# Weight conversion in the mixed steps: words combined ahead of the queries, next mask last, cast behind the numerators

## The chip, the cores and the metric

The kernel runs on one core of a Trainium2 chip. A core has TensorE (matrix products, into PSUM), VectorE, ScalarE and GpSimd (element-wise work), each with an instruction queue of its own that is worked off in order, and SyncE, whose queue issues most DMAs. An instruction waits on semaphores until what it needs is done and what it overwrites has been read; everything behind it on its engine waits as well. The metric is device time in microseconds. TensorE's clock was granted in full (2.4 GHz) through the stretch that the change touches.

## The reference

Three parts follow each other. First, attention with a feature map, for 4 batches, 8 heads, 576 tokens and head size 64:

```python
def phi(x):
    proj = x @ w_phi                       # 64 -> 128
    proj = proj - max(abs(proj))
    return concat(exp(proj), exp(-proj))   # 256 features
kv  = sum over tokens of phi(k) * v;   z = sum over tokens of phi(k)
out = (phi(q) @ kv) / (phi(q) @ z + 1e-6)
```

Its 2304 x 512 output goes to a mixture of 8 experts with one expert per token (argmax of `x @ w_gate`, a capacity per expert, two layers with relu, 1024 wide, gate weight on the result). Then comes a dense layer, `h = x @ w_in` (2048 wide), `g = h - tanh(h)`, `g @ w_out`. The dense layer's weights are handed over as 64-bit floats.

## The kernel before

**Steps.** The attention part works on 18 chunks of 128 tokens. `attention()` has a loop over steps `s`. Step `s` takes chunk `i = s` through the key side, chunk `j = s - 5` through the query projection (LAG is 5) and chunk `jt = s - 6` through transposition, exponentials and numerators. So keys and queries mix from step 5 to step 17. One key chunk passes through:

- `proj("k", i)`: 16 small products into a PSUM pair (`xb`, in early odd steps `yb`), L306;
- `sub("k", i)`, VectorE: the largest magnitude of each head (reduce, L314), then the subtract (L317);
- `kexp(i)`, ScalarE: the two exponentials, L328 and L329;
- `vgate(i)`, 16 products, and `vcopy`, ScalarE: value columns for the gate;
- `kv_step(i)` in the next step: 64 products (L358) that add to the key-value sums. At the end of a batch of 576 tokens `kv_evac` copies the sums to SBUF (ScalarE, L368).

A query chunk passes through `proj("q", j)` into `xb`, `sub("q", j)`, `trans` into `yb`, `qexp` (ScalarE, L396), `num` (64 products, L457, into `yb`) and the copies of denominators and numerators to SBUF (ScalarE, L474 and L475); `xstore` sends the numerators to DRAM. In steps 9 to 17 VectorE also runs pieces of the routing (`route1`, small operations) for the nine early chunks. In steps 10, 13 and 16 ScalarE's exponential of the routing (L510) stands ahead of the numerators' copy.

**Weight conversion.** Beside this, the steps convert the dense layer's weights, 13 pieces of 128 x 1024 numbers (`pieces`; `CV` maps step 4 to piece 0, step 16 to piece 12). A 64-bit number comes as two 32-bit words, and a piece passes through:

- `cv_load`: four DMAs of 256 KB into `raw` (two buffers), L119;
- scaling, `cv_mag`, ScalarE: exponent and top bits of the high word as a 32-bit float, into `a` (two buffers), L93;
- mask, VectorE: the sign bit of the high word, into `m` (one buffer), L98;
- shift, VectorE: `a` moved left by 3 bits, L100;
- combine, VectorE: the low word's top bits joined to it, L102;
- add, GpSimd: the sign joined to it, L106;
- `cv_hi`, the cast, ScalarE: the rounded high part of the weight, L277;
- `cv_lo`, GpSimd: the low part, `a` minus the high part, L280.

**What sets the order.** The program is in a manual schedule: each engine's queue holds its instructions in the order in which the loop writes them. Before the change, a step's mask and shift stand behind the key subtract, the combine behind the routing at the end, the cast and `cv_lo` of a piece one step later, and the scaling of the next piece at the very end of the step.

## Time and profile before

| | us |
|---|---|
| median of 3 runs (lowest, highest) | 668.98 (668.04, 670.8) |
| profiled execution | 670.01 |
| its span | 668.3 |
| busy: TensorE, VectorE, ScalarE, GpSimd | 637.6, 524.1, 411.4, 240.5 |

The span is the time from the first to the last instruction, about 1.7 us less than the device time. The mixed steps lie between 24 and 141 us, with the weight conversion from 23 to 140; the rest is the late query steps, the experts and the dense layer. An instruction's length in the trace runs from its start on the engine to its end; a wait for a semaphore stands before the start, as idle time. Successive VectorE instructions overlap by about 0.1 us.

### The profile page before, as it was taken

The numbers are of one execution on the slowest core, as the hardware profiler recorded it, in microseconds if no ns is written. First come the engines' busy times: TensorE is split into PE (matmuls) and PEld (weight loads), VectorE is DVE, ScalarE is ACT, GpSimd is POOL, SyncE is SP. The second block draws the span as 40 slices with busy tenths as digits, with TensorE's granted clock in tenths as the row PEclk, the third lists the DMA queues.
The fourth block names the chain that finished last, engine by engine and source line by source line (L and its number), as shares of the span: only waits on it lengthen the run. The fifth ranks groups of instructions, "written<-read, shape, count | busy, mean of one in ns | idle before, by whom it ended". The sixth has DMA issues, their size and how long they took to land. (4 is left out here: it accounts for less than half of the span.)

```text
span 668.3 us, 17411 instructions
## 1 busy us (share of the span) xinstructions
PE 637.6 (95%) x7107; PEld 620.9 (93%) x7107; DVE 524.1 (78%) x772; ACT 411.4 (62%) x720; POOL 240.5 (36%) x182
## 2 busy tenths in 40 slices
PE   7999899998998999999999999999999999999993
PEld 6889888888988999999999999999999999999992
DVE  4799999997867888989865548889975637888982
ACT  3688868786635576576644446567745526657661
POOL 1255564546000326433720113633460102543361
PEclk9999999999999999999999999999999999999998
DMA  8988886726446424402235501001315530100221
GB/s 284 298 282 296 258 275 209 226 74 218 143 145 199 158 95 167 136 4 87 68 97 166 161 6 44 26 1 44 97 28 159 165 108 1 41 13 1 88 70 40
DMA packets 44922, 83.14 MB, mean 124 GB/s; under 512 B 7281, under 2 KB 7921, under 8 KB 44833
## 3 DMA queue, kind: packets, MB, share of 16 engines
q1 hardware_dynamic: 39664, 68.99, 32.8%
q0 software_dynamic: 2624, 8.13, 4.2%
q10 hardware_dynamic: 2544, 4.82, 2.0%
q8 instruction: 58, 0.95, 0.6%
q14 instruction: 32, 0.25, 0.1%
HBM read 73.32 MB, written 13.31 MB: 130 GB/s over the span
## 5 line engine op out<-in xcount | busy, mean ns | idle before, releaser
L1030 POOL TENSOR_SCALAR al<-ut 128x576 fp32r<-128x576 f32 (+1 forms) x51 | 84.1, 1650 | 151.8 <-ACT ut L1026 83.0
L925 DVE TENSOR_TENSOR w<-raw,w 128x512 fp32r<-128x512 f32 x102 | 71.7, 719 | 45.8 <-ACT w L920 43.7
L920 ACT CAST w<-raw 128x512 fp32r<-128x512 f32 x102 | 61.6, 619 | 62.3 <-DMA raw<-w 30.4
L938 PE MATMUL xb<-xh,w_in_h 128*128 128x288 f32 x264 | 79.5, 301 | 1.3 <-ACT ut L1026 1.3
L940 PE MATMUL xb<-xh,w_in_l 128*128 128x288 f32 x264 | 78.3, 297 | 0.0
L939 PE MATMUL xb<-xl,w_in_h 128*128 128x288 f32 x264 | 78.2, 296 | 0.0
L1077 POOL DMA_INDIRECT out<-row,ids x18 | 20.6, 1146 | 115.7 <-DVE row L1075 77.6
L1017 DVE TENSOR_TENSOR al<-y,ah 128x576 fp32r<-128x576 f32 (+1 forms) x51 | 40.5, 795 | 24.8 <-ACT ah L1016 24.7
L1025 ACT COPY hs<-xb 128x576 f32<-128x576 f32 (+1 forms) x36 | 21.6, 600 | 58.7 <-DVE th L1048 28.6
L939 PE MATMUL kvb<-al,w_oa_h 128*128 128x288 f32 x180 | 53.5, 297 | 0.0
L940 PE MATMUL kvb<-ah,w_oa_l 128*128 128x288 f32 x180 | 53.2, 296 | 0.0
L938 PE MATMUL kvb<-ah,w_oa_h 128*128 128x288 f32 x180 | 53.2, 296 | 0.0
L1041 DVE SCALAR_TENSOR_TENSOR y<-y,ut 128x576 f32<-128x576 f32 (+1 forms) x51 | 41.3, 811 | 13.4 <-ACT y L1029 13.4
L938 PEld LDWEIGHTS xb<-xh,w_in_h 128*128 128x128 f32 x264 | 49.8, 189 | 1.4 <-ACT ut L1026 1.4
L1044 DVE SCALAR_TENSOR_TENSOR y<-y,y 128x576 f32<-128x576 f32 (+1 forms) x51 | 44.2, 867 | 7.3 <-ACT y L1031 5.9
L939 PEld LDWEIGHTS xb<-xl,w_in_h 128*128 128x128 f32 x264 | 49.7, 188 | 0.0
L940 PEld LDWEIGHTS xb<-xh,w_in_l 128*128 128x128 f32 x264 | 49.6, 188 | 0.0
L314 DVE TENSOR_REDUCE m<-xb 128x8 f32<-128x1024 f32 x33 | 40.3, 1221 | 11.2 <-PE xb L306 10.7
L1049 DVE COPY_PREDICATED y<-al,th 128x576 f32<-128x576 int32 (+1 forms) x51 | 42.8, 840 | 5.6 <-DVE th L1048 0.5
L1031 ACT ACTIVATE y<-ut,sq_b 128x576 f32<-128x576 f32 (+1 forms) x51 | 38.1, 748 | 13.5 <-DVE al L1017 11.7
L938 PE MATMUL yb<-xh,w 128*128 128x288 f32 x144 | 43.8, 304 | 0.7 <-DVE al L985 0.7
L938 PE MATMUL kvb<-ah,w 128*128 128x288 f32 x144 | 42.6, 296 | 1.8 <-ACT ah L984 1.0
(291 smaller groups left out, 2136.5 us busy)
## 6 DMA issues: line engine op xcount, KB each, us to landing
raw<-w SPq DMA_DIRECT2D x105, 256.0 KB, 3.1
raw<-win SPq DMA_DIRECT2D x32, 256.0 KB, 4.5
raw<-wout SPq DMA_DIRECT2D x20, 256.0 KB, 4.6
v<-v SPq DMA_DIRECT2D x16, 296.0 KB, 4.0
k<-kT SPq DMA_DIRECT2D x18, 256.0 KB, 4.6
vt<-vT SPq DMA_DIRECT2D x18, 256.0 KB, 3.7
q<-qT SPq DMA_DIRECT2D x18, 256.0 KB, 4.2
xs<-x SPq DMA_DIRECT2D x18, 256.0 KB, 3.9
```

Of the source, the lines that this page charges most:

```text
L314: nc.vector.tensor_reduce(out=m, in_=ps, axis=AX.X, op=ALU.max, apply_absolute_value=True)
L920: nc.scalar.copy(d[:, 0], t)
L925: eng.tensor_tensor(out=d[:, 1], in0=t, in1=d[:, 0].bitcast(F32), op=ALU.subtract)
L938: nc.tensor.matmul(o, ah, bh, start=first, stop=False, skip_group_check=True)
L939: nc.tensor.matmul(o, ah, bl, start=False, stop=False, skip_group_check=True)
L940: nc.tensor.matmul(o, al, bh, start=False, stop=last, skip_group_check=True)
L1017: nc.vector.tensor_tensor(out=AL[a][:, i], in0=y2[:, i], in1=AH[a][:, i].bitcast(F32), op=ALU.subtract)
L1030: nc.gpsimd.tensor_scalar(out=AL[a][:, i], in0=ut[:, i], scalar1=C2, scalar2=None, op0=ALU.is_gt)
L1031: nc.scalar.activation(out=y2[:, i], in_=ut[:, i], func=AF.Square, bias=sq_b[:, 1:2])
L1041: nc.vector.scalar_tensor_tensor(out=y1[:, i], in0=y1[:, i], scalar=T1, in1=ut[:, i], op0=ALU.add, op1=ALU.mult)
L1044: nc.vector.scalar_tensor_tensor(out=y2[:, i], in0=y2[:, i], scalar=T2, in1=y1[:, i], op0=ALU.add, op1=ALU.mult)
L1049: nc.vector.copy_predicated(y2[:, i], AL[a][:, i].bitcast(I32), th[:, i])
```

## The change

The mask leaves `cv_bits` and becomes `cv_mask`. In step `s`, shift, combine and GpSimd's add of the step's own piece stand together behind the key subtract, ahead of the queries. The scaling of the next piece stands behind the key exponentials, the mask of the next piece behind the routing as the step's last VectorE instruction, and the cast and `cv_lo` of the step's own piece behind the numerators, ahead of `vgate` and `vcopy`. The loads move too: a piece's first two DMAs are issued in the middle of a step (from step 4 on), the other two at the top of the next one.

```diff
--- before.py
+++ after.py
@@ -94,9 +94,6 @@
 
     def cv_bits(t, a, m=None):
 
-        if m is not None:
-            nc.vector.tensor_scalar(out=m, in0=t[:, :, 1], scalar1=SIGN, scalar2=None, op0=ALU.bitwise_and)
-            yield
         nc.vector.tensor_scalar(out=a, in0=a, scalar1=3, scalar2=None, op0=ALU.logical_shift_left)
         yield
         nc.vector.scalar_tensor_tensor(out=a, in0=t[:, :, 0], scalar=29, in1=a,
@@ -266,9 +263,13 @@
         def cv_mag(i):
             if i in raw:
                 a = cva[i] = cv.tile([P, NPC], I32, tag="a", name="a")
-                m = cvm[i] = cv.tile([P, NPC], I32, tag="m", name="m", bufs=1)
                 cvw[i] = a.bitcast(F32)
                 cv_size(raw[i], a)
+
+        def cv_mask(i):
+            if i in raw:
+                m = cvm[i] = cv.tile([P, NPC], I32, tag="m", name="m", bufs=1)
+                nc.vector.tensor_scalar(out=m, in0=raw[i][:, :, 1], scalar1=SIGN, scalar2=None, op0=ALU.bitwise_and)
 
         def cv_main(i):
             yield from cv_bits(raw.pop(i), cva.pop(i), cvm.pop(i))
@@ -761,7 +762,7 @@
             i, j, jt = s, s - LAG, s - LAG - 1
             jn = jt if s < SD else jt - 1 if s > SD else -1
             kk, qq, tt = i < NCH, 0 <= j < NCH, 0 <= jt < NCH
-            pc, pd = CV.get(s), CV.get(s - 1)
+            pc, pn = CV.get(s), CV.get(s + 1)
             since = {cs: s - (cs[-1] + LAG + 1) for cs in subs}
             if s == SK:
                 stk.close()
@@ -772,11 +773,9 @@
             if kk:
                 proj("k", i, xb if i > LAG or i % 2 == 0 else yb)
             if s >= LAG:
-                cv_load(s + 2 - LAG, 0, 1)
+                cv_load(s + 2 - LAG, 2, 3)
             if s + 2 < NCH:
                 ldk(s + 2)
-            if s >= LAG:
-                cv_load(s + 2 - LAG, 2)
             if kk:
                 if i < LAG:
                     vgate(i)
@@ -791,29 +790,28 @@
             if kk:
                 for _ in sub("k", i):
                     pass
-            bits = iter(()) if pc is None else cv_main(pc)
-            run(itertools.islice(bits, 2))
+            if pc is not None:
+                run(cv_main(pc))
             if qq:
                 proj("q", j, xb)
             if 0 <= j + 2 < NCH:
                 ldq(j + 2)
-            if s >= LAG:
-                cv_load(s + 2 - LAG, 3)
-            else:
+            if s < LAG:
                 for k in ((0, 1), (2, 3), (4, 5), (6,), (7,))[s]:
                     cv_load(k // 4, k % 4)
+            if s >= LAG - 1:
+                cv_load(s + 3 - LAG, 0, 1)
             if i - 1 in strad:
                 kv_second(i - 1)
             if i == NCH:
                 kv_step(i - 1)
                 first_ids()
-            if pd is not None:
-                cv_hi(pd)
-                cv_lo(pd)
             if kk:
                 kexp(i)
                 if i < LAG and i in strad:
                     vcopy(i, 1)
+            if pn is not None:
+                cv_mag(pn)
             wgen = iter(())
             if since[subs[-1]] == 3:
                 wgen = itertools.chain(route2(early), table(early))
@@ -836,14 +834,15 @@
                 smalls.append(fgen["u"])
             weave([], smalls)
             flush()
-            for _ in bits:
-                pass
+            if pn is not None:
+                cv_mask(pn)
             if 0 <= jn < NCH:
                 num(jn)
+            if pc is not None:
+                cv_hi(pc)
+                cv_lo(pc)
             if LAG <= i < NCH:
                 vgate(i)
-            if CV.get(s + 1) is not None:
-                cv_mag(CV[s + 1])
             if s == SK:
                 mo["first"]()
             if s + 2 < NCH:
```

The lines of the changed kernel are numbered a little differently: mask L272, shift L97, combine L99, reduce L315, subtract L318.

On VectorE, around steps 4 to 6, the queue before stood as follows; `raw_209` and `a_410` belong to piece 0, `raw_338` and `a_485` to piece 1, `yb` with L314 and L317 is the key chunk of step 5, and the first `xb` here is the first query chunk.

```order
L98 TENSOR_SCALAR m_411<-raw_209 128x1024
L100 TENSOR_SCALAR a_410<-a_410 128x1024
L102 SCALAR_TENSOR_TENSOR a_410<-raw_209,a_410 128x1024
L314 TENSOR_REDUCE m_540<-yb_85 128x8
L317 TENSOR_TENSOR d_542<-yb_85,m_540 128x1024
L98 TENSOR_SCALAR m_486<-raw_338 128x1024
L100 TENSOR_SCALAR a_485<-a_485 128x1024
L314 TENSOR_REDUCE m_594<-xb_84 128x8
L317 TENSOR_TENSOR d_596<-xb_84,m_594 128x1024
L102 SCALAR_TENSOR_TENSOR a_485<-raw_338,a_485 128x1024
```

The same stretch of VectorE's queue in the changed kernel, where `a_488` is piece 1's and `raw_480` piece 2's:

```order
L97 TENSOR_SCALAR a_410<-a_410 128x1024
L99 SCALAR_TENSOR_TENSOR a_410<-raw_209,a_410 128x1024
L272 TENSOR_SCALAR m_490<-raw_338 128x1024
L315 TENSOR_REDUCE m_544<-yb_85 128x8
L318 TENSOR_TENSOR d_546<-yb_85,m_544 128x1024
L97 TENSOR_SCALAR a_488<-a_488 128x1024
L99 SCALAR_TENSOR_TENSOR a_488<-raw_338,a_488 128x1024
L315 TENSOR_REDUCE m_601<-xb_84 128x8
L318 TENSOR_TENSOR d_603<-xb_84,m_601 128x1024
L272 TENSOR_SCALAR m_605<-raw_480 128x1024
```

The mask of piece 1 moved ahead of step 5's key reduce, and the combine of piece 1 from behind the first queries to ahead of them.

On ScalarE, step 6 before, from the query exponentials; `w_in_h` is the cast, `x` the numerators, `a_748` the scaling of the next piece.

```order
L396 ACTIVATE qp_639<-yb_85 128x1024 x2
L277 CAST w_in_h_65<-a_485 128x1024
L328 ACTIVATE kp_693<-d_676 128x8x128
L329 ACTIVATE kp_693<-d_676 128x8x128
L474 COPY dl_734<-yb_85 128x72
L475 COPY x_735<-yb_85 128x2x4x64
L337 CAST v1_152<-ones_123 128x8
L338 COPY v1_152<-sb_80 128x8x8
L93 ACTIVATE a_748<-raw_625 128x1024
```

The same step on ScalarE in the changed kernel (`a_701` is the next piece's scaling):

```order
L397 ACTIVATE qp_643<-yb_85 128x1024 x2
L329 ACTIVATE kp_698<-d_680 128x8x128
L330 ACTIVATE kp_698<-d_680 128x8x128
L93 ACTIVATE a_701<-raw_561 128x1024
L475 COPY dl_741<-yb_85 128x72
L476 COPY x_742<-yb_85 128x2x4x64
L278 CAST w_in_h_65<-a_599 128x1024
L338 CAST v1_152<-ones_123 128x8
L339 COPY v1_152<-sb_80 128x8x8
```

The scaling moved from behind `vcopy` to ahead of the numerators' copy, and the cast from ahead of the key exponentials to between that copy and `vcopy`.

## Rows read from the trace of the kernel before

In the first group the columns are: stretch, its length, then busy us and instructions (x) of TensorE's products, its weight loads, VectorE, ScalarE and GpSimd, the granted clock, the busy share of the DMA engines and GB/s. In the groups in order of time they are: start and length in us, engine (DVE is VectorE, ACT ScalarE, POOL GpSimd, PE TensorE), line, operation, output and inputs, shapes and types, count, and in brackets the idle time just before with what ended it.

**Rows 1.** Busy times of the mixed steps, by engine (columns above).

```profile
24.00:135.00 111.00, 103.61 (x2366) 96.22 (x2362) 105.81 (x132) 86.86 (x138) 59.01 (x27) 1.00 0.81 260
```

**Rows 2.** VectorE in order of time: start, length, engine, line, operation.

```profile
26.22 1.23 DVE L102 SCALAR_TENSOR_TENSOR a<-raw,a 128x1024 int32<-128x1024 int32 x1
27.36 1.22 DVE L314 TENSOR_REDUCE m<-yb 128x8 f32<-128x1024 f32 x1
...
30.00 0.69 DVE L98 TENSOR_SCALAR m<-raw 128x1024 int32<-128x1024 int32 x1
...
31.21 1.22 DVE L314 TENSOR_REDUCE m<-xb 128x8 f32<-128x1024 f32 x1
32.46 1.23 DVE L317 TENSOR_TENSOR d<-xb,m 128x1024 f32<-128x1024 f32 x1
33.61 2.23 DVE L102 SCALAR_TENSOR_TENSOR a<-raw,a 128x1024 int32<-128x1024 int32 x1
35.76 1.21 DVE L314 TENSOR_REDUCE m<-xb 128x8 f32<-128x1024 f32 x1
...
59.80 1.22 DVE L314 TENSOR_REDUCE m<-xb 128x8 f32<-128x1024 f32 x1
...
64.12 1.23 DVE L314 TENSOR_REDUCE m<-xb 128x8 f32<-128x1024 f32 x1 [0.56 <-PE xb L306]
...
67.06 2.14 DVE L501 TENSOR_TENSOR lgx<-dl,r 128x192 f32<-128x192 f32 x1
...
77.20 0.18 DVE L508 TENSOR_TENSOR ls<-lg,mx 128x24 f32<-128x24 f32 x1
...
89.96 1.15 DVE L98 TENSOR_SCALAR m<-raw 128x1024 int32<-128x1024 int32 x1
...
94.56 0.36 DVE L501 TENSOR_TENSOR lgx<-dl,r 128x192 f32<-128x192 f32 x1
...
103.24 1.45 DVE L508 TENSOR_TENSOR ls<-lg,mx 128x24 f32<-128x24 f32 x1
...
134.49 1.21 DVE L314 TENSOR_REDUCE m<-xb 128x8 f32<-128x1024 f32 x1
```

**Rows 3.** GpSimd in order of time, the same columns.

```profile
27.60 2.37 POOL L106 TENSOR_TENSOR a<-a,m 128x1024 int32<-128x1024 int32 x1 [5.70 <-DVE a L102]
32.38 2.37 POOL L280 TENSOR_TENSOR w_in_l<-a,w_in_h 128x1024 fp32r<-128x1024 f32 x1 [2.41 <-ACT w_in_h L277]
...
89.99 0.58 POOL L240 MEMSET v<- 64x584 f32 x1
```

**Rows 4.** ScalarE in order of time, the same columns.

```profile
28.91 1.17 ACT L93 ACTIVATE a<-raw 128x1024 f32<-128x1024 f32 x1 [1.43 <-DMA raw<-win]
...
31.23 1.07 ACT L277 CAST w_in_h<-a 128x1024 fp32r<-128x1024 f32 x1
...
64.36 1.25 ACT L368 COPY kvs<-kvb 128x438 f32<-128x438 f32 x3
...
77.42 0.22 ACT L510 ACTIVATE ls<-ls 128x24 f32<-128x24 f32 x1 [1.64 <-DVE ls L508]
...
77.65 0.59 ACT L475 COPY x<-yb 128x512 f32<-128x512 f32 x1
```

**Rows 5.** TensorE in order of time: three key projections (steps 6, 8 and 9).

```profile
33.74 1.16 PE L306 MATMUL xb<-small,k 64*128 64x128 f32 x16 [0.32 <-DVE d L317]
...
50.51 1.16 PE L306 MATMUL xb<-small,k 64*128 64x128 f32 x16
...
58.59 1.16 PE L306 MATMUL xb<-small,k 64*128 64x128 f32 x16
```

**Rows 6.** Tile view of the weight words: time from issue to landing.

```profile
DMA to landing us min/median/max: 2.9/4.5/6.6
```

**Rows 7.** ScalarE's waits, 24 to 125 us: total, times, longest.

```profile
ACT a L93 <- DMA raw<-win: 6.4, 4, 2.2
ACT a L93 <- DMA raw<-wout: 3.9, 1, 3.9
```

## The prediction

> **What bounds the kernel now.** I read first the busy times of the stretch that the change touches, the mixed steps from 24 to 135 us [rows 1]. VectorE is busy 105.8 of its 111.0 us and TensorE 103.6, while ScalarE has 24 us of room and GpSimd 52. The reader should see two engines near their limit at once, and 533 us of the span behind it that the change leaves alone. Then I read VectorE's instructions in order of time [rows 2], which show the order of the work in a step and where one instruction takes longer than its like; then what ran on GpSimd and ScalarE at those moments [rows 3, 4]; then TensorE's step starts [rows 5]; last, the landing of the weight loads and who waits for them [rows 6, 7].
>
> Three things stand in them. A plain step takes TensorE 8.08 us from one key projection to the next (50.51 to 58.59) [rows 5]. VectorE and TensorE pass one PSUM pair (xb) to and fro: the next key projection starts when the query subtract ends (32.46 + 1.23 = 33.69, projection 33.74) [rows 2, 5]. And VectorE instructions that read SBUF wait for GpSimd: the word combine at 33.61 takes 2.23 us instead of the 1.23 at 26.22, and it ends 1.09 us after GpSimd's subtract, which runs from 32.38 for 2.37 us [rows 2, 3]. The reduce at 27.36, which reads PSUM, keeps its 1.22 us beside GpSimd's add that starts at 27.60.
>
> **The change part by part, in the profiled execution's own time.** Its device time is 670.01 us, its span 668.3; the median of the three runs is 668.98. I add a difference to both.
>
> *The lead-in, steps 4 to 6.* The mask of piece 0 moves into step 3, where VectorE has idle time, so combine 0 starts a mask's 0.60 earlier, at 25.62, and GpSimd's add, 1.38 behind it as before, runs 27.0 to 29.4 [rows 2, 3]. Now the mask of piece 1 stands behind combine 0 and ahead of step 5's key reduce. There is one mask buffer, which that add reads, and step 4 has no queries whose reduce and subtract (1.25 + 1.23) could cover the add. The mask therefore starts at 29.4, and the load of piece 1 lets it go no earlier than 28.9 either (ScalarE's scaling of the same words started at 28.91, after waiting for a DMA) [rows 4]. Behind it are queued the key reduce, now at 30.05 instead of 27.36, and the whole of step 5. The shift is due 2.64 later (27.36 to 30.00), at 32.7. But the cast of piece 0 now stands in step 4 behind that scaling (28.91 + 1.17, then 1.07), so GpSimd's subtract of piece 0 runs about 31.25 to 33.6, and the shift, an SBUF instruction, waits for it: 0.9. Then 0.60 shift (half of 30.00 to 31.21), 1.14 combine (26.22 to 27.36), 1.25 reduce and 1.23 subtract of the queries: the key projection of step 6 starts at 37.9 instead of 33.74. The key reduce comes 1.21 behind it (58.59 to 59.80), at 39.1 instead of 35.76. Sum: **+3.35 us**. The second half of the lead-in's loss is that the combine, which before ran beside the key projection, now stands ahead of it.
>
> *Steps 6 to 8, no routing.* The round over xb is 1.21 (projection to reduce) + 2.6 (to the shift) + 0.60 + 1.14 + 1.25 + 1.28 (subtract to projection) = 8.08, as long as TensorE's own 8.08. The mask (0.6) lies beside the key projection. Three such steps are 24.3 with the small gaps; before, 35.76 to 59.80 is 24.04 [rows 2]. Sum: **+0.3**.
>
> *Steps 9 to 16.* The add now runs beside the query reduce and subtract, which read PSUM, so the late instructions of this stretch lose their extra: 67.06 (2.14; its like at 94.56 takes 0.36: 1.78), 89.96 (1.15 for 0.69: 0.46), 103.24 (1.45, its like at 77.20 takes 0.18: 1.27), and one like that at 112.63 (1.15) [rows 2]. That is -4.7. Twice a query reduce waited 0.56 for TensorE (64.12 and one like it); the combine now fills that: -1.1. The last mixed step has no mask: -0.6. What is late next is the shift. The cast stands behind the numerators' copy, and that stands behind the routing exponential or the copy of the key-value sums. In a step with that exponential it is 0.82 from the exponential to the end of the numerators' copy (77.42 to 78.24), then the cast's 1.07, so GpSimd's subtract starts 2.0 after the exponential and ends 4.35 after it [rows 4]. VectorE needs 0.3 to finish routing, 0.6 for the mask, 1.3 and 1.2 for the next key reduce and subtract, so its shift is due at 3.4: it waits 0.9. The copy of the sums (1.25 at 64.36) puts the cast as far back. Two steps of each kind: +3.6, and +0.6 for small overlaps elsewhere. Sum: **-2.2**.
>
> *The loads.* Each piece's four DMAs move half a step forward on SyncE. The first two still wait for the combine and now stand behind the query load and ahead of the vt load; the last two no longer wait for VectorE. The scaling moves forward by about as much, so I cost this at 0; what it can cost is the slower rival, what it can gain the faster one. *After the mixed steps*, step 17 has no cast and subtract any more, and its exponentials start without a waiting cast ahead of them: **-0.2**.
>
> In all +3.35 + 0.3 - 2.2 - 0.2 = **+1.2 us**: 671.2 against the profiled execution, 670.2 against the median.
>
> The one term without a row of its own is the shift's wait. The rows show a two-input combine wait for GpSimd's subtract, and a one-input mask, the shift's like, wait for a GpSimd memset: the mask at 89.96 ends 0.54 after the memset (89.99 + 0.58) [rows 2, 3]. Bounds: nothing, or a whole subtract (2.37) each time. I take the overlap that the order leaves, 0.9, by the mask's row, the nearest. Without any wait, the five shifts would come 4.5 us earlier on VectorE; but TensorE's 8.08 and the xb round let only half of that through, about 2.3 us, and the sum would be -1.1. With a whole subtract each it would be some +4.
>
> The Trainium skill, SBUF — State Buffer, "Who interferes with whom", says that a tensor_scalar between SBUF operands can enter a two-port mode and then contends with GpSimd, whose instruction holds the shared pair to its end. The trace agrees on the mask (1.15 us); no row here shows the shift beside a GpSimd subtract. By that rule the shift waits and the sum is +1.2; by the memset's row read narrowly, where only a memset would hold it, -1.1.
>
> **The rivals.**
> 1. *The start is cheaper and the waits go.* The shifts do not wait, and words half a step earlier free the exponentials. For it: ScalarE waited 6.4 + 3.9 us for weight words [rows 7], ahead of query exponentials. Against it: VectorE is back to back from 26.22 to 35.76 [rows 2], so there is nowhere to catch up the mask's wait. Price: lead-in without the shift's wait +2.45, +0.3, and -6.4 in steps 9 to 16: -3.6, so 665.4.
> 2. *A new round through the loads makes it slower.* The scaling now stands ahead of the numerators' copy on ScalarE, and it needs words that SyncE issues behind the store of the previous copy. The round is two issues (0.9), the landing, the scaling (1.17), the copy (0.8) and the handing over (0.1): 3.0 us plus the landing. It decides from a landing of 5.1 us in a plain step (8.1), 5.7 in one with routing (8.7). For it: landings reach 6.6, and one scaling waited 3.9 [rows 6, 7]. Against it: the median is 4.5, and these two loads now stand where the first two stood. At 6.0 us the round is 9.0: three plain steps lose 0.9 each and some others 0.3, +3.3, so 673.5; at 6.6 it is 9.6, three lose 1.5 and seven 0.9, +10.8: 681.
> 3. *It comes out even.* Steps 9 to 16 pay back the lead-in because the casts hold the shifts half as long: +1.8 instead of +3.6, so 668.4.
>
> **How the numbers follow.** My forecast, +1.2 with a range of its own of -0.5 to +3, has 0.45; rival 1 has 0.15, rival 2 0.2, rival 3 0.2. The predicted time is 670.2 us. The range that should hold it 8 times in 10 stops a little short of rival 1's 665.4 and takes in the mild form of rival 2: 666.0 to 674.0. A measurement of this kernel tells about 0.5% (3.3 us) from no change: under 665.6 or over 672.3. Faster is rival 1 and little else: 0.14. Slower is rival 2 and the upper edge of the forecast: 0.24. The rest, 0.62, is the same.
>
> **What would show it.** In the changed profile the mask of piece 1 on VectorE starts near 29.4, with the key reduce of step 5 at about 30; if that stands near 27.4, the lead-in was wrong. The key projection of step 6 starts near 37.9. No combine takes over 1.3 us, while shifts of 1.3 to 1.9 us (mask and shift had 0.69 before) stand in the steps after an exponential or a copy of the sums; if they stay at 0.69, the +4.2 in steps 9 to 16 was wrong. Scaling that waits for a DMA in most steps, with the numerators' copy late behind it, would be rival 2. The key reduce of step 17 stands near 135.9 (134.49 before). The forecast is wrong as a whole if that instant moves by more than 3.3 us, or if the time from there to the end, 533.8 us before, changes by more than 1.

## The result and the profile after

The changed kernel takes **675.45 us** (median of 5 runs, 674.11 to 676.15); the kernel before, beside it, 668.21 (668.04 to 670.8). The ratio is 1.010, with a 95% interval of 1.008 to 1.012: slower by 7 us, outside the predicted range. The profiled execution took 674.11 us, its span is 672.4.

To see where the time went I cut the mixed steps at TensorE's key projections, which every kernel here has. All numbers are us from one start to the next, each from one profiled execution:

| kernel | steps 4-5 | 6-8 | 9-13 | 14-16 | sum |
|---|---|---|---|---|---|
| before | 12.61 | 24.85 | 45.39 | 27.86 | 110.71 |
| changed | 16.33 | 27.10 | 43.68 | 28.99 | 116.10 |
| difference | +3.72 | +2.25 | -1.71 | +1.13 | +5.39 |

The spans of these two executions differ by 4.1 us only, where the medians differ by 7.2: the profiled execution before is 1.8 above its median, the one after 1.3 below. Their 4.1 are 0.56 ahead of the table's first start, the table's 5.39, and -1.9 behind its last. Neither the first nor the last of these is read here as the work of the change. The first 20 us hold the same work in both kernels, and they differ between executions: step 4's projection starts at 21.13 before, at 21.69 here and at 23.61 in the repeat below, with a granted clock of 1.00, 0.70 and 0.50 from 12 to 16 us. So stretches are compared in what follows, and instants on the clock of the span only with that in mind.

First VectorE in the lead-in, in order of time; the rows that answer to it are [rows 2]. The columns of all rows in order of time are those of the rows before.

```profile
26.09 1.23 DVE L99 SCALAR_TENSOR_TENSOR a<-raw,a 128x1024 int32<-128x1024 int32 x1
29.88 0.69 DVE L272 TENSOR_SCALAR m<-raw 128x1024 int32<-128x1024 int32 x1 [2.56 <-POOL a L103]
30.49 1.22 DVE L315 TENSOR_REDUCE m<-yb 128x8 f32<-128x1024 f32 x1
...
32.95 1.36 DVE L97 TENSOR_SCALAR a<-a 128x1024 int32<-128x1024 int32 x1
34.35 1.22 DVE L99 SCALAR_TENSOR_TENSOR a<-raw,a 128x1024 int32<-128x1024 int32 x1
35.49 1.22 DVE L315 TENSOR_REDUCE m<-xb 128x8 f32<-128x1024 f32 x1
...
39.96 1.22 DVE L315 TENSOR_REDUCE m<-xb 128x8 f32<-128x1024 f32 x1 [1.23 <-PE xb L307]
```

The mask of piece 1 (29.88) starts after VectorE has idled 2.56 us, and the key reduce of step 5 follows it at 30.49 instead of 27.36. The shift (32.95) takes 1.36, and the combine (34.35) now stands ahead of the query reduce (35.49). GpSimd and ScalarE at the same time [rows 3, 4]:

```profile
27.47 2.37 POOL L103 TENSOR_TENSOR a<-a,m 128x1024 int32<-128x1024 int32 x1 [5.01 <-DVE a L99]
31.40 2.36 POOL L281 TENSOR_TENSOR w_in_l<-a,w_in_h 128x1024 fp32r<-128x1024 f32 x1 [1.56 <-ACT w_in_h L278]
```

```profile
29.23 1.17 ACT L93 ACTIVATE a<-raw 128x1024 f32<-128x1024 f32 x1 [1.28 <-DMA raw<-win]
30.30 1.03 ACT L278 CAST w_in_h<-a 128x1024 fp32r<-128x1024 f32 x1
```

The add ends at 29.84, just ahead of the mask; the words of piece 1 were there by 29.23, when the scaling that waited for them starts. TensorE, three key projections and the transposes behind the first (steps 6, 8, 9) [rows 5]:

```profile
38.02 1.90 PE L307 MATMUL xb<-small,k 64*128 64x128 f32 x16 [3.35 <-DVE d L318]
39.85 1.96 PE L391 MATMUL yb<-ident,d 128*128 128x128 f32 x8
...
55.78 1.16 PE L307 MATMUL xb<-small,k 64*128 64x128 f32 x16
57.50 1.09 PE L391 MATMUL yb<-ident,d 128*128 128x128 f32 x8 [0.56 <-ACT x L476]
...
65.12 1.16 PE L307 MATMUL xb<-small,k 64*128 64x128 f32 x16 [0.43 <-DVE d L318]
```

The first projection of step 6 comes after 3.35 us of idleness and takes 1.90 instead of 1.16, the transposes 1.96 instead of 1.09: from 38 to 42 us the granted clock is 0.57, nearly the lower of the two levels (1.2 GHz). The columns of the next two rows are those of [rows 1], the row that the first answers to:

```profile
24.00:135.00 111.00, 100.34 (x2242) 92.50 (x2240) 100.34 (x120) 85.68 (x132) 58.45 (x26) 0.98 0.80 255
38.00:42.00 4.00, 3.98 (x32) 3.43 (x34) 2.63 (x3) 1.42 (x4) 2.36 (x2) 0.57 1.02 306
```

From 24 to 135 us VectorE is busy 5.5 us less than before, with 120 instructions instead of 132: the steps are longer, so less of the work lies in the same stretch. Around the start of step 8, ScalarE (still with the end of step 7), GpSimd and VectorE:

```profile
55.67 1.20 ACT L93 ACTIVATE a<-raw 128x1024 f32<-128x1024 f32 x1 [1.52 <-DMA q<-qT]
...
56.84 0.61 ACT L476 COPY x<-yb 128x512 f32<-128x512 f32 x1
57.32 1.08 ACT L278 CAST w_in_h<-a 128x1024 fp32r<-128x1024 f32 x1
```

```profile
58.48 2.40 POOL L281 TENSOR_TENSOR w_in_l<-a,w_in_h 128x1024 fp32r<-128x1024 f32 x1 [2.69 <-ACT w_in_h L278]
```

```profile
59.46 1.96 DVE L97 TENSOR_SCALAR a<-a 128x1024 int32<-128x1024 int32 x1
```

This is a chain. The scaling waits 1.52 for a DMA; the wait is put down to the query load issued at 53.22, but its own last words, issued at 49.98, may as well have come last. The numerators' copy stands behind it, and TensorE's transposes wait for the copy (57.50). The cast follows the copy, then comes GpSimd's subtract, and the next step's shift, beside it, takes 1.96 instead of 0.69. The same start of a chain stands in step 15:

```profile
128.13 1.13 ACT L93 ACTIVATE a<-raw 128x1024 f32<-128x1024 f32 x1 [1.64 <-DMA raw<-wout]
```

Last, the end of the mixed steps, in step 17, VectorE and GpSimd:

```profile
139.01 2.35 DVE L526 TENSOR_TENSOR r<-r,mx 128x24 f32<-128x24 f32 x1
...
141.47 1.21 DVE L315 TENSOR_REDUCE m<-xb 128x8 f32<-128x1024 f32 x1
```

```profile
138.94 2.38 POOL L281 TENSOR_TENSOR w_oa_l<-a,w_oa_h 128x1024 fp32r<-128x1024 f32 x1 [1.16 <-ACT w_oa_h L278]
```

A routing multiply of 24 numbers per partition takes 2.35 (the same line at 118.86, with no GpSimd work beside it, 0.18) beside the subtract of the last piece and ends with it, ahead of the key reduce that answers to 134.49 [rows 2]. Below, "held" means this: an instruction takes longer than its like beside one of GpSimd's, and ends with it or just behind it. ScalarE's and VectorE's waits from 24 to 135 us (total, times, longest):

```profile
ACT a L93 <- DMA raw<-wout: 3.1, 2, 1.6
...
DVE m L272 <- POOL a L103: 2.6, 1, 2.6
ACT a L93 <- DMA raw<-win: 2.4, 3, 1.3
...
ACT a L93 <- DMA q<-qT: 1.5, 1, 1.5
```

Scaling waits less for DMAs in total than before (7.0 us; before, 10.3 [rows 7], which is also its sum up to 135 us), but now the numerators' copy stands behind it.

### The profile page after: what moved, and what is told of

The parts are those of the page before. It is cut to its first block, busy times and chain, and to the rows that moved or that the text cites. A ratio compares the mean times of both kernels' runs of the same rounds, so it can differ in the third digit from the quotient of the medians.

```text
span 672.4 us, 17424 instructions
## 1 busy us (share of the span) xinstructions
PE 640.5 (95%) x7107; PEld 623.4 (93%) x7107; DVE 524.5 (78%) x772; ACT 412.8 (61%) x720; POOL 240.1 (36%) x182
## 5 line engine op out<-in xcount | busy, mean ns | idle before, releaser
L315 DVE TENSOR_REDUCE m<-xb 128x8 f32<-128x1024 f32 x33 | 40.2, 1219 | 15.8 <-PE xb L307 15.8
L359 PE MATMUL kvb<-v,kp 128*64 128x74 f32 x1152 | 42.6, 232 | 3.8 <-ACT kp L330 1.3
L359 PEld LDWEIGHTS kvb<-v,kp 128*64 128x64 f32 x1152 | 39.5, 139 | 7.3 <-issue 2.7
```

Of the source, the lines that this page charges most:

```text
L315: nc.vector.tensor_reduce(out=m, in_=ps, axis=AX.X, op=ALU.max, apply_absolute_value=True)
L359: nc.tensor.matmul(kvb[bank][64 * a:64 * a + 64, col * NKV:col * NKV + VS], kp[i][:, 4 * g + hp, s, 64 * a:64 * a + 64], vt[:, 2 * hp + g, :],
```

## The experiments

Each ratio is against the kernel before on the same chip (its medians there 668.6 to 669.2), with its 95% interval. Stretches are those of the table above, each from one profiled execution.

**The changed kernel again**, on a chip of the experiments.

> The changed kernel itself, on the chip of the experiments. All theories: 675.4 as before, ratio 1.008 to 1.012; under 1.006 would mean that the gains read from the kernels with one part put back (0.3 to 0.5%) were the chip's, not the edits'.

676.77 us, ratio 1.0127 [1.0111, 1.0144]: the changed kernel stands at 1.010 to 1.013. Stretches 15.93, 27.41, 43.16, 30.62. The end differs from the first profile: in step 15 the scaling waits 2.58 instead of 1.64, the last subtract comes later (142.15), and the routing multiply ahead of it is not held:

```profile
141.94 0.18 DVE L526 TENSOR_TENSOR r<-r,mx 128x24 f32<-128x24 f32 x1
```

**One part put back at a time.** The mask of piece 1 behind the key subtract:

```
+ if s == 5: cv_mask(pc)          # ahead of cv_main; not at the end of step 4
```

> The changed kernel with the mask of piece 1 back behind step 5's key subtract; all else as changed. Theory A (the lead-in stall costs its own length and then a lower TensorE clock): the key reduce of step 5 comes near 27, TensorE does not stand still before step 6's key projection, that projection starts near 34.5 instead of 38.0 and takes 1.16 instead of 1.90, and the time is 4 to 5 us under the changed kernel's 675.45: about 670.8. Rival (the steps behind catch up whatever the start): under 1.5 us gained, 674 to 675.5.

672.79, ratio 1.0063 [1.0033, 1.0092]: between the theory and the rival. Step 5's key reduce comes at once, but GpSimd's subtract (33.15, 2.39 long) now holds the combine of piece 1, which takes 3.27 us from 33.36: steps 4-5 take 15.24. Some 1 us of the lead-in came back; behind the mask stands another instruction that is held.

Products that keep TensorE busy ahead of step 6:

```
+ if s == 6: 30 products of zeros into yb     # ahead of proj("k", 6)
```

> The changed kernel with 30 extra products of zeros into the free yb pair ahead of step 6's key projection; they fill the time in which TensorE waits, and are read by nobody. Theory A: the granted clock stays full, projection and transposition of step 6 take 1.16 and 1.09 again, and 1.5 to 2 us come back: about 673.7. Rival (the clock was low only by chance in the profiled run): no change, 675 to 676.

674.42, ratio 1.0075 [1.0049, 1.0101]. Step 6 takes 8.09 here, 9.68 and 9.64 in the two profiles of the changed kernel. But with the last piece's cast put back (below), TensorE was as idle as in the changed kernel and kept its clock:

```profile
37.91 1.16 PE L307 MATMUL xb<-small,k 64*128 64x128 f32 x16 [3.36 <-DVE d L318]
39.00 1.09 PE L391 MATMUL yb<-ident,d 128*128 128x128 f32 x8
```

So the clock sometimes falls after the idle time, which costs 1.6 us in step 6, and sometimes does not. The time is under the repeat's, but its interval overlaps the first measurement's; how much of the change's cost this is stays open.

Cast and low part of the last piece back in step 17:

```
- cv_hi(12); cv_lo(12)            # step 16, behind the numerators
+ cv_hi(12); cv_lo(12)            # step 17, ahead of kexp
```

> The changed kernel with the cast and the low part of the last piece back in step 17, ahead of its key exponentials. Theory A (GpSimd's last subtract holds a small routing multiply of step 16, 2.35 us instead of 0.18): that multiply takes 0.18 and about 2 us come back: 673.4. Rival (step 17 then waits for the cast as before the change, and the gain is lost there): 675 to 676.

674.05, ratio 1.0079 [1.005, 1.0108]. The multiply takes 0.18 again, as it does in the repeat without this edit. The median is 1.4 to 2.7 us lower, but the interval overlaps the changed kernel's first one: a gain is not shown.

The scaling back at the end of its step:

```
- cv_mag(pn)                      # behind kexp
+ cv_mag(pn)                      # behind vcopy, last on ScalarE
```

> The changed kernel with the scaling of the next piece back at the end of the step, behind vcopy; loads stay as changed. Theory A (scaling that waits for its words holds up the numerators' copy, the cast and so the shift two or three times): no numerators' copy behind a waiting scaling, the shift of step 8 at 0.69 instead of 1.96, and 1 to 3 us come back: about 673.5. Rival (the scaling then pushes the query exponentials, which costs as much): 675 to 677.

671.88, ratio 1.0052 [1.0028, 1.0076], clear of the changed kernel's interval by either measurement: 3.6 to 4.9 us less. No scaling waits for a DMA any more, though the loads stay in their new order, and steps 6-8 take 24.24, three times 8.08; step 8 on TensorE:

```profile
53.23 1.16 PE L307 MATMUL xb<-small,k 64*128 64x128 f32 x16
...
61.31 1.16 PE L307 MATMUL xb<-small,k 64*128 64x128 f32 x16
```

Step 8 divides all profiles of this record with the early combine and the cast behind the numerators: with the scaling early there it takes 9.24 to 11.51 us (seven profiles), with the scaling late 8.08 to 8.59 (ten). But steps 14-16 took 32.02, because a routing operation of step 16 is held now, TensorE waits 2.57, and then its own products are slow, with a granted clock of 0.71 from 130 to 134 us (VectorE, GpSimd, TensorE):

```profile
125.42 2.28 DVE L509 TENSOR_TENSOR ls<-lg,mx 128x24 f32<-128x24 f32 x1
```

```profile
125.28 2.38 POOL L281 TENSOR_TENSOR w_oa_l<-a,w_oa_h 128x1024 fp32r<-128x1024 f32 x1 [1.42 <-ACT w_oa_h L278]
```

```profile
130.82 1.31 PE L307 MATMUL xb<-small,q 64*128 64x128 f32 x16 [2.57 <-DVE d L318]
132.06 3.73 PE L458 MATMUL yb<-kvs,qp 128*64 128x74 f32 x64
```

So the mixed steps of this profile are only 1.1 us shorter than in the changed kernel's first and 2.1 shorter than in its repeat. The rest of the medians' difference stands, in these profiles, ahead of step 4 and behind step 17, where this edit moves nothing: how much of the 3.6 to 4.9 is the scaling's is not shown.

**Several parts.** All three put back, and then the low part of piece 0 on VectorE as well:

> Three parts of the change go back at once: the scaling to the end of its step, the mask of piece 1 behind step 5's key subtract, the cast and low part of the last piece into step 17. The combine ahead of the queries, the masks as last VectorE work of the other steps and the cast behind the numerators' copies stay. Theory (three separate costs, each seen in its own stretch): the gains add up, 1.1 in the lead-in, 1.3 to 2.9 in steps 6 to 8, about 1.5 in steps 9 to 17, so 4 to 5.5 less than the changed kernel: ratio to before 0.997 to 1.003, some 669. Rival (they are one wait that turns up elsewhere when it is taken away, as GpSimd's subtract did with the routing multiply of step 15 when the scaling went late): no better than with the scaling late alone, 671 to 673, with a new VectorE row held over 2 us in front of a key projection.

672.1, ratio 1.0053 [1.0032, 1.0074]: the rival. Nothing is gained over the late scaling alone. The lead-in is as long (15.93), since ScalarE's cast of piece 0, ahead of piece 1's scaling, now waits 1.9 for the add; and the routing operation of step 16 takes 2.29, held again.

> As the kernel with three parts back, and the low part of piece 0 on VectorE behind step 5's query subtract instead of on GpSimd. Theory (in the lead-in GpSimd's subtract of piece 0 holds the combine of piece 1, 3.27 for 1.23): the combine takes 1.23, step 6's key projection starts 1.5 to 2 earlier than with three parts back, and the time is 1.5 to 2 less than that kernel's, at or under before's. Rival: step 6 waits for something else by then (piece 1's words or its scaling), and VectorE's own 1.3 for the low part is added to step 5: no gain or 1 more.

671.58, ratio 1.0039 [1.0024, 1.0055]. The combine takes 1.22 and the lead-in 14.68, but its shift waits 1.40 for piece 1's scaling behind that cast. The median is 0.5 lower where 1.5 to 2 were expected, and the intervals do not separate that from nothing.

**What the holding itself costs.** GpSimd's subtract over 256 of the 1024 numbers, the rest of the low parts preset:

```
- subtract(out=low, in0=a, in1=high)
+ subtract(out=low[:, 0:256], in0=a[:, 0:256], in1=high[:, 0:256])
```

> The changed kernel with GpSimd's subtract cut to a quarter of its words, the other three quarters of each low part preset to zero in the first microseconds, where VectorE and GpSimd are idle: it leaves out three quarters of the low parts. Theory (the subtract holds VectorE's shifts, 5.6 over their 0.69 in all, and the routing multiply of step 17, 2.2 over): shifts at 0.69, the multiply at 0.18 to 0.3, and of the 7.8 about 4 come back, since part of the holding lies beside the waits for TensorE: 671 to 672. Rival 1 (the order itself costs, the scaling's wait for its words above all): shifts short, but the steps as long as before, 674 to 676. Rival 2 (all of it on the path): 667 to 668.

> As the kernel with the quarter subtract, and the scaling back at the end of its step: leaves out the same three quarters of the low parts. Theory (the two costs are one chain: the scaling's wait pushes the cast and the subtract behind it into the next step's shift): 669 to 671, no more than 1.5 under the better of the two kernels that have one of the edits. Rival (two independent costs): their gains add, 3.5 and 4 under the changed kernel's 675.4, so 667 to 668.

674.65, 1.0077 [1.0046, 1.0108], with the scaling early; 672.62, 1.0048 [1.003, 1.0067], with it late. Every shift is at 0.69 and no routing multiply is held, yet the first is only 0.8 and 2.1 us below the two measurements of the changed kernel, and the second no better than the late scaling alone. These times do not price the holding, though, because the preset takes time of its own. VectorE is at it until 8.37 us, and the first reduce of the program stands behind it, at 8.29 (5.35 to 6.56 in all other profiles):

```profile
2.02 3.93 DVE L282 MEMSET w_in_l<- 128x768 f32 x5
6.06 2.31 DVE L282 MEMSET w_oa_l<- 128x768 f32 x3
8.29 1.16 DVE L320 TENSOR_REDUCE m<-xb 128x8 f32<-128x1024 f32 x1
```

The stretches leave the preset out. With the scaling late, steps 9-13 take 41.69 (42.81 with the whole subtract) and steps 14-16 29.29 (32.02). With it early they take 42.05 (43.68 and, in the repeat, 43.16) and 28.52 (28.99 and 30.62), but in step 8 the scaling now waits 2.76, and the step takes 11.51 (9.34 and 9.69). So the holding does cost something in steps 9 to 16, some 2 to 4 us by one profile each. The lead-in stays at 15.65 and 15.63: that is not the holding.

**A buffer of its own for the mask of piece 1**, which asks what the 2.56 is.

```
- m = cvm[1] = cv.tile(... name="m", bufs=1)
+ m = cvm[1] = first half of the qp tile, free until step 6
```

> The changed kernel with a buffer of its own for piece 1's mask (free room that the queries use only from step 6); nothing else is changed. Theory (in the lead-in the mask of piece 1 waits 2.56 for GpSimd's add to leave the only mask buffer, and step 5's key maximum stands behind it): no such wait, from step 4's key projection to step 6's 13.8 to 14.4 instead of 16.3, time 2 to 2.6 less than the changed kernel's. Rival (what stands behind holds anyway: GpSimd's subtract of piece 0 beside the combine of piece 1, as when the mask was put behind the key subtract, 3.27 for 1.23): 15.2 there, 1 less.

676.83, ratio 1.0132 [1.0113, 1.015]: no gain, and not for the rival's reason. VectorE:

```profile
28.66 1.49 DVE L276 TENSOR_SCALAR qp<-raw 128x1024 int32<-128x1024 int32 x1 [1.58 <-DMA raw<-win]
30.08 1.21 DVE L319 TENSOR_REDUCE m<-yb 128x8 f32<-128x1024 f32 x1
...
32.53 1.22 DVE L97 TENSOR_SCALAR a<-a 128x1024 int32<-128x1024 int32 x1
```

Freed of the add, the mask waits 1.58 for its words, and then takes 1.49 beside the add. The key reduce stands at 30.08, hardly earlier than the 30.49 of the changed kernel. The mask's place ahead of that reduce is too early in itself: its words land some 1.3 us after the instant at which the reduce starts in the kernel before (27.36).

**One part alone, on the kernel before**: combine and add ahead of the query projection.

```
- run(itertools.islice(bits, 2))   # mask, shift
+ run(bits)                        # mask, shift, combine, add
```

> The kernel before, with one part of the change alone: the combine and GpSimd's add stand ahead of the query projection, right behind the mask and the shift; loads, scaling, mask and cast as before. Theory (VectorE has 1.2 more ahead of the query's maximum, 2.2 where the subtract holds the combine; in steps 5 and 6 VectorE sets the pace, in the others TensorE): step 6's key projection 1.2 to 2.2 later, the others even: 669.5 to 671, ratio 1.002 to 1.004. Rival 1 (the maximum's delay counts in every step, with the xb buffer as the round's bound): 8 or more, ratio over 1.01. Rival 2 (the combine is no longer stretched, and the masks either): 667 to 668.

**681.88**, ratio 1.0208 [1.0192, 1.0224]: +13.3, the first rival in size. Stretches 13.81, 26.03, 50.41, 31.96. TensorE, ScalarE, GpSimd and VectorE of steps 9 to 11:

```profile
61.64 1.16 PE L306 MATMUL xb<-small,k 64*128 64x128 f32 x16 [0.44 <-DVE d L317]
...
70.32 1.16 PE L306 MATMUL xb<-small,k 64*128 64x128 f32 x16 [0.46 <-DVE d L317]
...
80.30 1.16 PE L306 MATMUL xb<-small,k 64*128 64x128 f32 x16 [1.03 <-DVE d L317]
83.60 1.97 PE L390 MATMUL yb<-ident,d 128*128 128x128 f32 x8 [2.13 <-ACT x L475]
85.50 4.22 PE L358 MATMUL kvb<-v,kp 128*64 128x74 f32 x64
```

```profile
64.06 1.19 ACT L93 ACTIVATE a<-raw 128x1024 f32<-128x1024 f32 x1 [2.02 <-POOL w_in_l L280]
...
82.73 0.22 ACT L510 ACTIVATE ls<-ls 128x24 f32<-128x24 f32 x1 [4.13 <-DVE ls L508]
```

```profile
59.34 2.37 POOL L106 TENSOR_TENSOR a<-a,m 128x1024 int32<-128x1024 int32 x1 [3.98 <-DVE a L102]
61.67 2.35 POOL L280 TENSOR_TENSOR w_in_l<-a,w_in_h 128x1024 fp32r<-128x1024 f32 x1
```

```profile
80.90 1.79 DVE L508 TENSOR_TENSOR ls<-lg,mx 128x24 f32<-128x24 f32 x1
```

Three costs at once. The round over the PSUM pair xb has the mask and the combine in it: 8.68 a step (61.64 to 70.32) instead of 8.08. The add, now early, stands ahead of the previous piece's subtract on GpSimd's queue, and the next scaling waits 2 us for the buffer that this subtract reads. And the late subtract holds the routing operations ahead of ScalarE's exponential, 4.13 us of waiting at 82.73, with TensorE idle behind it (2.13) and slow after (4.22 for 2.27, the granted clock is 0.50 from 84 to 88 us). Step 11 takes 13.11.

**Casts back in the next step**, with scaling late and mask 1 put back: of piece 0 and the last, of 0 and the last four, of all.

```
- cv_hi(pc); cv_lo(pc)                     # behind the numerators
+ cv_hi(CV[s - 1]); cv_lo(CV[s - 1])       # ahead of kexp, for the pieces named
```

> The kernel with three parts back, and piece 0's cast and low part, too, in the step behind it (step 5, ahead of the keys' exponentials, where the kernel before has them); only pieces 1 to 11 are cast behind the numerators. Theory (in the lead-in it is the cast of piece 0 that holds ScalarE: it waits 1.9 there for GpSimd's add, and behind it stand piece 1's scaling, the copies of the key-value sums, and so TensorE's next 64 products): from step 4's key projection to step 6's 13 to 14.2, against 15.9 with three parts back and 12.6 before; time 1.5 to 2 less than with three parts back, ratio 1.002 to 1.003. Rival (GpSimd's subtract of piece 0 then stands beside the combine of piece 1, which is now ahead of the query projection, and holds it 2 longer): 15 to 16 there, no gain.

> As the one before, and the casts and low parts of the last four pieces in the step behind theirs, so that no subtract of GpSimd stands beside the routing multiplies of steps 15 to 17. Theory: no routing multiply over 0.4, steps 15 to 17 together 27.9 to 29, against 32.0 with three parts back and 27.9 before; time 2 to 3.5 less than the kernel ahead of it, at or under before's: ratio 0.996 to 1.000. Rival (the subtract holds something else there, a combine or a reduce of step 15 or 16, and the stretch stays as long): no more than 0.5 less.

> All casts and low parts in the step behind theirs, the scaling late, the mask of piece 1 behind the key subtract: of the change only the combine ahead of the query projection and the mask as the last VectorE work of a step stay, with the loads in their new order. Theory (the cast behind the numerators gives nothing between steps 7 and 13, where a step takes TensorE's 8.08): within 1 of the kernel with five casts back. Rival 1 (GpSimd's subtract early in a step holds the combine, as it did twice in the kernel before, now ahead of the query projection): 2 to 4 more. Rival 2 (the late cast costs there as well): 1 to 2 less.

Two casts: 670.73, 1.0034 [1.0022, 1.0047], with the lead-in at 14.06, as its theory said, and 1.4 less time than with three parts back. Five casts: 673.32, 1.0075 [1.0059, 1.0092]; its theory failed: the subtracts of the later casts hold three other routing operations (2.31, 2.12 and, in step 17, 2.28). All casts: **686.88**, 1.027 [1.0254, 1.0285], against 672.1 (1.0053) with all but the last behind the numerators. The cast behind the numerators is the part that makes the early combine bearable: 14.8 us.

**Each part where it pays.** Mask 1 behind the key subtract, piece 0 cast in step 5 with its low part on VectorE, the last cast back, the scaling late up to step 12 and early from 13:

```
+ if pn is not None and s >= 13: cv_mag(pn)   # ahead of the numerators' copy
+ if pn is not None and s < 13:  cv_mag(pn)   # last on ScalarE
```

> The combine ahead of the queries, the mask last and the cast behind the numerators kept for pieces 1 to 11; mask 1 behind the key subtract, piece 0 cast in step 5 with its low part on VectorE behind the query subtract, the last piece cast a step later, and the scaling late up to step 12, early from step 13 on, where the changed kernel's stretch was 3 shorter than with late scaling. Theory (the losses sit in separate stretches and add): from step 4's key projection to step 9's 38 to 39.5 (before 37.5, changed 43.4), step 9 to 14 42.8 (before 45.4), step 14 to 17 28.5 to 29.5 (before 27.9): even with before, ratio 0.997 to 1.001. Rival (something outside these stretches costs too): the stretches as said, and still 1.003 or more.

**667.64**, ratio 0.9994 [0.9979, 1.0008]: level with the kernel before, as its theory said. Stretches 13.27, 24.61, 42.80, 29.10. TensorE in steps 6 and 7:

```profile
34.50 1.16 PE L308 MATMUL xb<-small,k 64*128 64x128 f32 x16 [1.16 <-DVE d L319]
...
42.95 1.16 PE L308 MATMUL xb<-small,k 64*128 64x128 f32 x16 [0.30 <-DVE d L319]
```

So the losses sit in the stretches in which they were located, and with them repaired the change gives 2.6 in steps 9-13 and loses 1.9 in steps 4-5 and 14-16. Three variants of steps 13 to 17 (scaling late in all and the last two casts back; scaling early in 13 and 14 and the last two casts back; scaling early in 14 alone):

> As the one before, but the scaling late in all steps, and the last two pieces cast a step later. Theory (the routing multiply of step 16 is held by the subtract of the last but one piece, cast behind the numerators of step 15): no multiply of step 16 over 0.4, step 14 to 17 28.5 to 30 instead of 32.0; ratio 0.998 to 1.002. Rival (the subtract, a step later, holds another routing operation, as when four pieces were cast later): 30 to 32, ratio 1.002 to 1.004.

> As the mix, but the scaling early in steps 13 and 14 alone, and the last two pieces cast a step later. Theory (the scaling ahead of the numerators' copies waits for its words in step 15, and GpSimd's subtract of the last but one piece holds a routing operation of step 16 or 17): step 14 to 17 28 to 28.5, time 0.6 to 1 less than the mix: ratio 0.996 to 0.999. Rival (the later subtract holds a routing operation of step 17, 2.3 for 0.2, which the stretch hides): as the mix or up to 1.5 more.

> As the mix, but the scaling early in step 14 alone. Theory: step 14 to 17 28 to 28.5, ratio 0.996 to 0.999. Rival (late scaling in step 15 brings back the multiply of step 16 held by the subtract, 2.3 for 0.2, as with the scaling late alone): 31 to 32 there, ratio 1.002 to 1.004.

670.47, 1.0031 [1.0008, 1.0054]; 671.3, 1.0023 [1.0008, 1.0037]; 671.22, 1.0033 [1.0019, 1.0046]. None is better. Steps 14-16 took 28.92, 29.00 and 32.57; in the last the routing operation of step 16 is held again (2.03). In the first two another one is held instead, in step 17 (L515, 2.28). No version beats the kernel before. The time from step 17's key projection to the end was 532.2 to 537.7 in all these profiles (536.5 before, 534.6 changed), one each, so a difference of 2 us there is not explained here.

No run gives the kernel before the new order of the loads alone, and none moves the mask alone. What those two parts give or cost by themselves stays open.

## Why the prediction was wrong

- **The lead-in was right in size.** The projection of step 6 was predicted 4.16 later (33.74 to 37.9); it came 3.72 later counted from step 4's projection, 4.28 on the clock of the span (38.02). The mask (29.88 for 29.4), the key reduce (30.49 for 30.05) and the shift's wait (0.67 for 0.9) came as written. Of its two reasons, the busy mask buffer is not needed: with a second buffer the words' landing, and the add beside the mask, put the key reduce in nearly the same place. What the prediction left out is TensorE's clock, which fell after the longer wait in both profiles of the changed kernel.
- **The step that failed is "The loads", costed at 0.** Scaling waited less in total (7.0 us for 10.3), but its place had changed: the numerators' copy, the cast, the subtract and the next shift now stand behind it. In the seventeen profiles named above, step 8 took 9.24 to 11.51 us with the scaling early and 8.08 to 8.59 with it late, and the kernel with the scaling put back is 3.6 to 4.9 us faster by the medians, of which its profile shows 1.1 to 2.1 in the mixed steps. Rival 2 named this scaling and this copy, but with a price by landing times near 6 us and only as TensorE's round; the chain through the cast and the next step's shift was not in it. The loads by themselves did no harm: in their new order, with the scaling late, no scaling waits for a DMA, where the waits were 10.3 us before.
- **Steps 6 to 8**, predicted at +0.3 from key reduce to key reduce, came out at +2.33 (26.37 for 24.04). By projections they take 27.10, and 24.24 would be three times 8.08: 1.6 of the difference lies in step 6 with the lower clock, 1.26 in step 8 with the scaling's wait. With the scaling late, all three take 8.08, as the round of the prediction has it.
- **Steps 9 to 16, predicted at -2.2, are the second miss**: to the key reduce of step 17 they came out near +0.4 (-1.71, +1.13, and 1.03 more from step 17's projection to its reduce, 3.68 for 2.65). The gain was there: no combine or mask is stretched any more, and steps 9-13 are 1.7 shorter, 2.6 with late scaling. The shifts' waits came to about the size given: +3.6 and +0.6 predicted, 3.70 measured over the 0.69 of six shifts, though partly by luck: 2.58 in the four steps behind an exponential or a copy of the sums (10, 11, 14, 15), 1.12 in steps 12 and 13, which the prediction does not name. Two losses were not in the sum. Scaling waited ahead of the numerators' copy in steps 12 (1.45) and 15 (1.64). And where the prediction says that step 17 has no cast and subtract any more, the subtract of the last piece ran there from 138.94 and held a routing multiply for 2.17; in the repeat it did not.
- **The two signs of a forecast that is wrong as a whole both came.** The key reduce of step 17 stands at 141.47, 6.98 later (1.4 predicted, 3.3 allowed). The time from there to the end is 530.9 for 533.8, where 1 was allowed: 1.03 of it is the reduce's own delay behind the multiply, and the rest is not explained.
- **Slips in the working.** The gains of steps 9 to 16 leave out the mask at 98.54 (1.03 for 0.69) of the kernel before. By the same halving as for no wait, a whole subtract at each shift gives a sum of +4.9, not some +4. And the case that the shifts do not wait has two prices, -1.1 under the sum and -3.6 in rival 1. None of these changes the account.
- The Trainium skill, SBUF — State Buffer, "Who interferes with whom", says that a VectorE instruction in a two-port mode, or with two SBUF inputs beside a GpSimd one that reads SBUF, and the GpSimd instruction block each other at a shared port pair, whoever comes first for its whole length. The trace agrees on the shift (1.96 at 59.46, which ends 0.54 after the subtract) and on a multiply of 24 numbers (2.35 at 139.01); what that costs the kernel depended on what else was waiting.
- **What the prediction did not ask**: whether the parts need each other. The early combine alone costs 13.3, and the cast behind the numerators gives 14.8 back; a sum over edits made one at a time has no term for either.

## What to carry to other kernels

When an instruction that waits for a DMA moves forward on its engine, list what now stands behind it, up to the next step's work on other engines; the total of its waits may fall and the kernel still be slower. A stretched instruction in the trace is a cost only as far as nothing else was late beside it. Shorten its holder to price it, and then compare the stretches in which it stands, not only the whole time: the shortening itself can cost time elsewhere, as the preset did here. Where several moves belong together, price each alone and all together, since one may only repay what another costs. And look at a second profile of the same kernel before you explain a single held instruction: the multiply of step 17 was held in one and free in the other.

## What the runs showed of the hardware

- After TensorE had stood idle before step 6, the granted clock fell in some profiles and not in others: after 3.35 us in the changed kernel (0.57 from 38 to 42 us), after 3.36 in its repeat and with the second mask buffer, after 3.06 and 2.05 with the quarter subtracts; not after 3.36 with the last cast back, nor after 2.66 with mask 1 put back, nor after 2.33 with the scaling late.
- A GpSimd subtract of 1024 numbers (2.37 us) held VectorE operations of 24 numbers for up to nearly its whole length (2.35 us in step 17 of the changed kernel, 2.28 in step 16 with the scaling late; 0.18 without it). The wait stands inside the held instruction's own length, not as idle time before it.
